# A three-stage kernel whose instruction order becomes a table over single instructions, with a named buffer for each place of a ring

## The chip, the core and the metric

The kernel runs on one core of one Trainium2 chip. The metric is the device time of one execution in microseconds (us), the median of several runs. The core has five queues of instructions that run beside each other, each in its own order: TensorE (PE, matrix products), VectorE (DVE), ScalarE (ACT), GpSimd (POOL) and SyncE (SP, which here issues all DMA transfers). An instruction that waits holds back everything behind it on its own queue.

## What is computed

An attention with a memory term, then two feed-forward networks, on 4 batches, 8 heads, 576 tokens and 64 values per head, so 2,304 rows of 512:

```python
scores = scale * q @ k.T, causal; a = softmax(scores); local = a @ v
q_p = phi(q); mem_out = (q_p @ M_prev) / (q_p @ z_prev + 1e-6)
x = sigmoid(beta) * mem_out + (1 - sigmoid(beta)) * local    # rows of 512
h = x @ w_in;  g = 0 | (h+1)**2/4 | h  by range;  x = g @ w_out        # 512 -> 2048 -> 512
h = x @ w2_in; g = max(h, 0) + alpha * min(h, 0); x = g @ w2_out
```

The weights arrive as 64-bit floats. Accuracy is kept by splitting: each operand of a product is a 16-bit high part and a 16-bit rest, and each product is done as three 16-bit products.

## The kernel before

Work is cut by batch b (0 to 3), by pairs of heads pr (0 to 3) and by two chunks of 288 tokens. The sections have short names: p0 prepares batch 0 (norms and scales), a0A1 is the attention of batch 0, pair 1, its first row blocks (B the later ones, C all), w1i, w1o, w2i and w2o are the four weights, u00 is the first product of the first network (batch 0, chunk 0, eight steps u00.0 to u00.7), d00 its second product, f00 the second network with steps f00.o0 to f00.o3 for its second product.

A weight comes in 16 raw pieces of 128x1024 words (512 KB). DVE and ACT turn two pieces into `w_t` (line 687 on), a product with ones gives a bound, then `copy` (line 516) makes the 16-bit high part on ACT, DVE or POOL, and `rest` (line 534) the 16-bit rest: on DVE one SCALAR_TENSOR_TENSOR, on POOL two instructions, a TENSOR_SCALAR over the source and a TENSOR_TENSOR. The same two helpers split q, k, v and the probabilities. In the networks, `split` does `copy` and `combine` (line 531, a subtraction on POOL or DVE) for the tile g.

All instructions are recorded first. `schedule` (line 273) then plays a list scheduler over estimated costs: each named part has a rank in the table RANK, each helper that could run on several engines may have its engine fixed in the table HOME, else the scheduler chooses, and the order in which it starts the instructions is the order in which they are issued (`run`, line 420). Tiles of one tag share a ring of equal places (`BUFS`, line 459: four for x, five for g, three for tmp, two for qk); a tile takes the place that is free when its turn comes. All instructions are issued from line 426.

Of the kernel before, what the change touches and what calls it, by code (L numbers as in the profile page):

```python
# [11 lines left out]
F32 = mybir.dt.float32  # L12
F32R = mybir.dt.float32r
F16 = mybir.dt.float16
# [29 lines left out]
class _Op:  # L44
    __slots__ = ("section", "first", "ways", "users", "before", "tiles", "size", "wide", "rows", "port", "key")
# [15 lines left out]
class _Pool:  # L61


    def __init__(self, plan, pool, name, bufs):
        self.plan, self.pool, self.name, self.bufs = plan, pool, name, bufs

    def tile(self, shape, dtype, tag=None, name=None, bufs=None):
        bufs = bufs or self.bufs
        if tag is None:
            ap = self.pool.tile(shape, dtype, name=name)  # L70
        else:
            ap = self.pool.tile(shape, dtype, tag=tag, name=name, bufs=bufs)
        self.plan.tiles[ap.tensor.name] = _Tile((self.name, tag or name), bufs)
        return ap


class _Tile:
    def __init__(self, group, bufs):
        self.group, self.bufs = group, bufs
        self.writes, self.reads, self.users = [], [], []  # L80


class Plan:

    NEAR, FAR, LAND = 0.14, 0.2, 0.8

    SLACK = 0.5

    def __init__(self, tc):
        self.tc = tc
        self.tiles = {}
        self.ops = []
        self.first = False
        self.joined = None
        self.turns = defaultdict(int)
        self.name = self.section = "c"  # L100

    def part(self, name):

        self.name = f"{self.section}.{name}"

    def pool(self, ctx, name, bufs, space=None):
        kw = {} if space is None else {"space": space}
        return _Pool(self, ctx.enter_context(self.tc.tile_pool(name=name, bufs=bufs, **kw)), name, bufs)

    @contextmanager  # L110
    def ahead(self):
        self.first = True
        yield
        self.first = False
# [8 lines left out]
    def either(self, *ways):  # L123
# [7 lines left out]
        self.turns[self.name] += 1  # L131
        first.key = f"{self.name}:{self.turns[self.name]}"
        if first.key in HOME:
            first.ways = {HOME[first.key]: first.ways[HOME[first.key]]}

    @staticmethod
    def cost(eng, method, out, ins, kw):

        w = max(math.prod(a.shape[1:]) for a in ((out, *ins) if method == "tensor_reduce" else (out,)))
        psum = any(a.space == PSUM for a in (out, *ins))  # L140
        scalars = sum(isinstance(kw.get(k), bass.AP) for k in ("scale", "bias", "scalar", "scalar1", "scalar2"))
        accum = kw.get("accum_out") is not None
        if eng == "act":
            extra = 0.054 + 0.094 * (scalars > 1) if psum else 0.1 * (scalars > 0)
            apart = 0.05 * any(a.ap[-1][0] == 2 for a in ins)
            return 0.1 + w / 1200 + extra + 0.09 * accum + apart
        if eng == "dve":
            if method == "tensor_tensor_reduce":
                return 0.078 + w / 960 + 0.06 * scalars
            if method == "reciprocal":  # L150
                return 0.09 + 0.006 * w
            rate = 1.04
            if not psum and not accum and method in ("tensor_scalar", "tensor_copy"):
                rate = 0.62 if out.dtype == F32 else 0.67 if out.dtype != I16 else 0.85
            small = 0.1 if w <= 8 else 0
            return 0.068 + w * rate / 1000 + 0.06 * max(psum, scalars) + small
        if method == "tensor_tensor":
            even = any(a.ap[-2][0] == 0 or a.ap[-1][0] == 0 for a in ins)
            return 0.148 + w * (1.667 if even else 1.886 if out.dtype == F16 else 2.103) / 1000
        if method == "tensor_scalar":  # L160
            return 0.161 + w / 1200 + 0.083 * (scalars > 0)
        return 0.3

    @staticmethod
    def two_ports(method, outs, ins, kw):

        big = [a for a in ins if a.space != PSUM and mybir.dt.size(a.dtype) == 4 and math.prod(a.shape[1:]) > 1]
        if method in ("tensor_scalar", "tensor_copy"):
            return bool(big) and outs[0].space != PSUM and kw.get("accum_out") is None
        return method in ("tensor_tensor", "scalar_tensor_tensor") and len(big) > 1  # L170

    @staticmethod
    def box(ap):

        n = mybir.dt.size(ap.dtype)
        dims = ap.ap
        if ap.space == bass.MemoryType.DRAM:
            lo = ap.offset
            return 0, 1, [(lo * n, (lo + 1 + sum(s * (c - 1) for s, c in dims)) * n, 0, 0)]
        row = dims[0][0]  # L180
        p0, lo = divmod(ap.offset, row) if row else (0, ap.offset)
        starts, size, step, width = [lo * n], n, 0, n
        for s, c in sorted(dims[1:], key=lambda d: abs(d[0])):
            if s == 0 or c == 1:
                continue
            if s * n > size and c * len(starts) <= 32:
                starts = [x + i * s * n for x in starts for i in range(c)]
                continue
            if s * n > size and len(starts) == 1:
                step, width = (s * n, size) if not step else (0, 0)  # L190
            size += s * (c - 1) * n
        return p0, p0 + dims[0][1], [(x, x + size, step, width) for x in starts]

    @staticmethod
    def overlap(a, b):
        def meet(r, q):
            if r[0] >= q[1] or q[0] >= r[1]:
                return False
            if r[2] and r[2] == q[2]:
                d = (q[0] - r[0]) % r[2]  # L200
                return d < r[3] or d + q[3] > r[2]
            return True

        return a[0] < b[1] and b[0] < a[1] and any(meet(r, q) for r in a[2] for q in b[2])

    def add(self, eng, method, fn, args, kw):
        aps = [a for a in args if isinstance(a, bass.AP)]
        outs = [kw[k] for k in ("out", "accum_out") if isinstance(kw.get(k), bass.AP)]
        ins = [v for k, v in kw.items() if isinstance(v, bass.AP) and k not in ("out", "accum_out")]
        if not outs:  # L210
            outs = aps[:1]
            aps = aps[1:]
        elif aps:
            raise ValueError(method)
        ins += aps
        if self.joined:
            op = self.joined
        else:
            op = _Op()
            op.section, op.first = self.name, self.first  # L220
            op.ways, op.users, op.before, op.tiles, op.rows, op.port, op.key = {}, [], 0, [], [], False, None
            self.ops.append(op)
            if self.joined is False:
                self.joined = op
        calls, cost = op.ways.setdefault(eng, ([], []))
        calls.append((fn, args, kw))
        if eng == "pe":
            if method == "transpose":
                cost.append(2 * P)
                op.rows.append(1.0)  # L230
            else:
                n = math.prod(kw["rhs"].shape[1:])
                whole = kw["rhs"].dtype == F32


                cols = math.prod(kw["lhsT"].shape[1:])
                if kw["lhsT"].shape[0] == 64 and whole:
                    cost.append(2 * n + 348)
                elif kw["lhsT"].shape[0] == 64:
                    cost.append(0.5 * n + (228 if kw["start"] and len(cost) < 2 else 6))  # L240
                elif cols == 64:
                    cost.append((2 if whole else 0.5) * n + (228 if kw["start"] and len(cost) < 2 else 6))
                else:
                    cost.append(max(4 * n, 300) if whole else n)
                op.rows.append(kw["lhsT"].shape[0] / P * (min(n, P) / P if whole else 1))
        elif eng == "dma":
            op.size = math.prod(outs[0].shape) * mybir.dt.size(outs[0].dtype)
            if "transpose" in method:
                op.size = -op.size
# [6 lines left out]
        for ap, writes in [(a, False) for a in ins] + [(a, True) for a in outs]:  # L256
            t = self.tiles.get(ap.tensor.name)
            if t is None:
                continue
# [1279 lines left out]
```

## Time and profile before

| | |
|---|---|
| time, median of 3 runs | 1032.7 us (1026.01 to 1033.71) |
| span of the profiled execution | 1028.9 us; its own time is not listed apart, the median lies 3.8 us above its span |
| instructions | 20,943 |
| PE busy | 934.1 us, 91% |
| DVE, ACT, POOL busy | 682.0, 525.0 and 357.0 us |
| chain that ended last | PE 52%, DVE 20%, ACT 9%, DMA 8%, POOL 5% |

The profile gives busy time by engine, tables by stretch of time, the instructions in order of time, and the chain of work that ended last, followed back from the last instruction. Every instruction has the line of the one place that issues it, so tiles tell them apart: `ring` and `w1o_raw` are raw weights, `s` scores, `e` the exponentials, `sm` their sums, `h` and `g` the network's inner values. `x3` counts instructions.

### The profile page before, as it was taken

The numbers are of one execution on the slowest core, as the hardware profiler recorded it, in microseconds if no ns is written. First come the engines' busy times: TensorE is split into PE (matmuls) and PEld (weight loads), VectorE is DVE, ScalarE is ACT, GpSimd is POOL, SyncE is SP. The second block draws the span as 40 slices with busy tenths as digits, with TensorE's granted clock in tenths as the row PEclk, the third lists the DMA queues.
The fourth block names the chain that finished last, engine by engine and source line by source line (L and its number), as shares of the span: only waits on it lengthen the run. The fifth ranks groups of instructions, "written<-read, shape, count | busy, mean of one in ns | idle before, by whom it ended". The sixth has DMA issues, their size and how long they took to land.

```text
span 1028.9 us, 20943 instructions
## 1 busy us (share of the span) xinstructions
PE 934.1 (91%) x8215; PEld 703.2 (68%) x8215; DVE 682.0 (66%) x1748; ACT 525.0 (51%) x1091; POOL 357.0 (35%) x382
## 2 busy tenths in 40 slices
PE   1557979998999999999899999999999999999998
PEld 0334656766766666776577777777777777777776
DVE  5977887799888899999879988872241313142230
ACT  7867777466655667356655555653232323132220
POOL 3433334476547566374524424131120200100010
PEclk9955889999999999999999999999999999999999
DMA  8934413457734957455565444321100000000000
GB/s 311 340 109 139 171 57 109 117 131 164 173 98 109 209 121 177 64 153 157 100 161 161 151 142 137 118 79 38 36 12 13 12 18 7 24 7 18 12 13 24
DMA packets 135171, 107.80 MB, mean 105 GB/s; under 512 B 98464, under 2 KB 113312, under 8 KB 135072
## 3 DMA queue, kind: packets, MB, share of 16 engines
q1 hardware_dynamic: 135072, 106.47, 36.8%
q8 instruction: 64, 1.05, 0.5%
q14 instruction: 35, 0.29, 0.1%
HBM read 70.27 MB, written 9.44 MB: 77 GB/s over the span
## 4 chain that ended last, share of the span: by engine, by line
PE 52%; DVE 20%; ACT 9%; DMA 8%; POOL 5%; issue 4%; SPq 1%; ACTq 0%; DVEq 0%; POOLq 0%
PE h L426 24%; PE o L426 18%; PE y L426 5%; DVE p L426 3%; DVE u L426 2%; DVE d L426 2%; DVE e L426 2%; PE px L426 2%; DMA w2i_raw<-in_w2i 2%; DVE g L426 2%; DMA pt<-p 2%; ACT e L426 2%; PE s L426 2%; SPq L426 1%; DMA qn<-in_qn 1%
## 5 line engine op out<-in xcount | busy, mean ns | idle before, releaser
L426 PE MATMUL h<-x,w1i 128*128 128x288 f16 x1536 | 203.6, 290 | 10.8 <-DVE u L426 10.1
L426 PE MATMUL y<-g,w1o 128*128 128x288 f16 x1536 | 202.4, 288 | 2.9 <-DVE u L426 2.5
L426 PE MATMUL h<-yt,w2i 128*128 128x288 f16 x1536 | 195.8, 286 | 2.9 <-ACT u L426 2.9
L426 PE MATMUL o<-g,w2o 128*128 128x288 f16 x1536 | 194.4, 286 | 0.1
L426 PEld LDWEIGHTS <-w1i 128*128 128x128 f16 x1536 | 148.3, 99 | 58.0 <-DVE u L426 15.3
L426 PEld LDWEIGHTS <-w1o 128*128 128x128 f16 x1536 | 146.1, 98 | 51.8 <-issue 10.1
L426 PEld LDWEIGHTS <-w2i 128*128 128x128 f16 x1536 | 150.3, 98 | 41.4 <-issue 3.7
L426 PEld LDWEIGHTS <-w2o 128*128 128x128 f16 x1536 | 150.2, 98 | 38.2 <-issue 0.4
L426 DVE SCALAR_TENSOR_TENSOR u<-u,al 128x288 f32<-128x288 f32 x128 | 64.7, 531 | 151.1 <-ACT u L426 151.0
L426 POOL TENSOR_TENSOR g<-u,g 128x576 f16<-128x576 f32 x50 | 70.1, 1403 | 154.9 <-ACT g L426 128.9
L426 ACT ACTIVATE u<-h,sa 128x288 f32<-128x288 f32 x128 | 59.2, 498 | 120.9 <-PE h L426 111.8
L426 POOL TENSOR_SCALAR g<-u 128x576 f16<-128x576 f32 x31 | 23.3, 753 | 253.6 <-DVE u L426 156.9
L426 DVE TENSOR_TENSOR g<-u,g 128x576 f16<-128x576 f32 x78 | 62.1, 798 | 70.8 <-ACT g L426 63.6
L426 ACT ACTIVATE e<-e,mxt 128x576 f32<-128x576 f32 (+4 forms) x160 | 88.1, 552 | 39.5 <-DVE mxt L426 36.9
L426 ACT ACTIVATE d<-d,bu,su 128x576 f32<-128x576 f32 x64 | 55.4, 865 | 51.2 <-DVE d L426 40.4
L426 PE MATMUL s<-qk 64*128 64x288 f16 (+9 forms) x528 | 66.8, 335 | 14.8 <-DVE mxt L426 8.5
L426 ACT ACTIVATE g<-u 128x576 f16<-128x576 f32 x75 | 51.1, 681 | 52.8 <-DVE u L426 36.4
L426 ACT ACTIVATE oe<-o,osc 128x288 f32<-128x288 f32 x32 | 16.0, 500 | 109.5 <-PE o L426 100.0
L426 DVE TENSOR_SCALAR d<-h,lim 128x576 f32<-128x576 f32 x64 | 55.6, 869 | 6.9 <-PE h L426 6.5
L426 DVE SCALAR_TENSOR_TENSOR p<-e,sm,p 128x192 f16<-128x192 f32 (+4 forms) x84 | 57.2, 707 | 1.1 <-ACT p L426 0.9
L426 DVE CUSTOM_DVE_ANT_0 e<-s,mask,qs 128x64 f32<-128x64 f32 (+4 forms) x120 | 54.7, 480 | 4.0 <-PE s L426 3.7
L426 DVE SCALAR_TENSOR_TENSOR u<-h,sd,d 128x576 f32<-128x576 f32 x64 | 52.0, 812 | 6.3 <-ACT d L426 5.3
(229 smaller groups left out, 1225.7 us busy)
## 6 DMA issues: line engine op xcount, KB each, us to landing
ring<-in_w1i SPq DMA_DIRECT2D x16, 512.0 KB, 6.2
w1o_raw<-in_w1o SPq DMA_DIRECT2D x16, 512.0 KB, 4.0
w2i_raw<-in_w2i SPq DMA_DIRECT2D x16, 512.0 KB, 4.1
w2o_raw<-in_w2o SPq DMA_DIRECT2D x16, 512.0 KB, 4.3
qr<-in_qk SPq DMA_DIRECT2D x24, 288.0 KB, 3.3
qn<-in_qn SPq DMA_DIRECT2D x16, 320.0 KB, 3.4
vc<-in_vc SPq DMA_DIRECT2D x16, 320.0 KB, 4.5
y<-ye SPq DMA_DIRECT2D x32, 144.0 KB, 2.4
```

Of the source, the lines that this page charges most:

```text
L426: fn(*args, **kw)
```

## The change

The recorded instructions are the same. The scheduler, its costs, RANK and HOME go. A table ISSUE lists the 3,795 recorded steps by number in the order in which they are issued, with a letter (a, v, g for ACT, DVE, POOL) where a step can run on several engines. A table PLACES gives each tile of a ring its place by name, as a buffer of its own with a fixed width.

```diff
-    def schedule(self, ops):
-        ...
-    def run(self, sections):
-        order, _ = self.schedule(...)
+    def run(self):
+        engines = dict(a="act", v="dve", g="pool")
+        order = ISSUE.split()
+        ...
+            for t in order:
+                op = self.ops[int(t.rstrip("avg"))]
+                eng = engines[t[-1]] if op.key else next(iter(op.ways))
+                for fn, args, kw in op.ways[eng]:
+                    fn(*args, **kw)
 ...
     def tile(self, shape, dtype, tag=None, name=None, bufs=None):
-        bufs = bufs or self.bufs
+        words, order = PLACES[f"{self.name}.{tag}"]
+        key = (tag, order[self.made[tag]])
+        self.made[tag] += 1
+        if key not in self.places:
+            self.places[key] = self.pool.tile([P, words], F32, tag="".join(key), name="".join(key), bufs=1)
 ...
-RANK = """
-w1i0.m1 w1i0.s0 s1 m1.0 p0.n c w1i0.m0 w1i1.m0 l p0.0 p0.2 a0A1.1 a0A1.2 a0A0.1 w1i2.m0 a0A0.0 w1i1.s1 a0A0.2 s0 p0.1
+    "sb.x": (1152, "3210011011001311231320300023320132013"),
+ISSUE = """
+1 40 5 2 6 0 34 22 13 70 7 41 72 42 43 69 23 8 9 35 44 186 36 28 24 10 37 1304 71 25 92a 11 45 26 76 12 18 91 187 38
```

Of the 980 steps that can run on several engines, 495 get another engine than before. Of the subtractions for g (`combine`), 41 go from DVE to POOL and 17 from POOL to DVE. Of the rests of weights, 12 go from POOL to DVE and 2 the other way. The order is close to the old one in the large and differs in the small nearly everywhere. Three places follow.

The first is SP's queue near the program's start, its DMA transfers 19 to 27; qk0_0_1 and qk0_0_0 are q and k of batch 0, pairs 1 and 0.

```order
L426 DMA w1o_raw0_0_324<-in_w1o 128x1024 [waits DMAHW2_49]
L426 DMA vc0_3_89<-in_vc 128x640 [waits DMAHW3_49,Activation_49]
L426 DMA w1o_raw0_1_325<-in_w1o 128x1024 [waits DMAHW4_49]
L426 DMA w1o_raw1_0_326<-in_w1o 128x1024 [waits DMAHW5_49]
L426 DMA qk0_0_1_176<-in_qk 128x2x320 [waits DMAHW6_49]
L426 DMA vf0_0_2_214<-in_vp 128x256 [waits DMAHW7_49]
L426 DMA vf0_0_2_214<-in_vp 64x384 [waits DMAHW0_49]
L426 DMA vf0_0_2_214<-in_vp 64x3x128 [waits DMAHW1_49]
L426 DMA qk0_0_0_137<-in_qk 128x2x320 [waits DMAHW2_49]
```

In the change the names are those of the places (wb0 to wb3 hold raw pieces of w1i, tmp0 a piece of vc); these are its transfers 12 to 22, where qk0 and qk1 are the same two loads of pairs 1 and 0.

```order
L135 DMA wb1_114<-in_w1i 128x1024 [waits DMAHW3_49]
L135 DMA tmp0_87<-in_vc 128x640 [waits DMAHW4_49,DVE_49]
L135 DMA qk0_146<-in_qk 128x2x320 [waits DMAHW5_49]
L135 DMA wb2_115<-in_w1i 128x1024 [waits DMAHW6_49]
L135 DMA wb3_116<-in_w1i 128x1024 [waits DMAHW7_49]
L135 DMA wb2_115<-in_w1i 128x1024 [waits DMAHW0_49]
L135 DMA vf0_145<-in_vp 64x384 [waits DMAHW1_49]
L135 DMA tmp2_88<-in_vc 128x640 [waits DMAHW2_49,DVE_49]
L135 DMA tmp0_87<-in_vc 128x640 [waits DMAHW3_49,Activation_49]
L135 DMA qn4_181<-in_qn 128x640 [waits DMAHW4_49]
L135 DMA qk1_128<-in_qk 128x2x320 [waits DMAHW5_49]
```

The load for pair 1 moved from the 23rd place on the queue to the 14th: four pieces of w1i, three of w1o and three of vc that stood ahead of it now stand behind it, and the load for pair 0 moved from 27th to 22nd.

The second place is SP's queue some thirty transfers later. Before, the fourth to sixth pieces of w1o wait for DVE, with q and k of batch 0, row block 3 (qk0_3_1) between them.

```order
L426 DMA qk0_0_3_254<-in_qk 128x2x320 [waits DMAHW5_49,PE_49]
L426 DMA vc1_2_518<-in_vc 128x640 [waits DMAHW6_49,DVE_49]
...
L426 DMA kc1_1_523<-in_qk 128x576 [waits DMAHW3_49,Activation_49]
L426 DMA w1o_raw1_1_327<-in_w1o 128x1024 [waits DMAHW4_49,DVE_49]
L426 DMA qk0_3_1_411<-in_qk 128x576 [waits DMAHW5_49,PE_49]
L426 DMA w1o_raw2_0_340<-in_w1o 128x1024 [waits DMAHW6_49,DVE_49]
```

In the change the same stretch reads so; x0, x1 and g0 to g3 here hold raw pieces of w1o, wb1 the last piece of w1i, and qk0 the load of pair 3.

```order
L135 DMA x1_171<-in_w1o 128x1024 [waits DMAHW7_49]
L135 DMA qk0_146<-in_qk 128x2x320 [waits DMAHW0_49,PE_49]
L135 DMA wb1_114<-in_w1i 128x1024 [waits DMAHW1_49]
...
L135 DMA g0_169<-in_w1o 128x1024 [waits DMAHW4_49]
L135 DMA vf1_127<-in_vp 64x384 [waits DMAHW5_49]
L135 DMA g1_162<-in_w1o 128x1024 [waits DMAHW6_49]
L135 DMA g2_166<-in_w1o 128x1024 [waits DMAHW7_49]
L135 DMA g3_168<-in_w1o 128x1024 [waits DMAHW0_49]
L135 DMA tmp2_88<-in_vc 128x640 [waits DMAHW1_49,Activation_49]
...
L135 DMA x1_171<-in_w1o 128x1024 [waits DMAHW3_49,DVE_49]
```

Four pieces of w1o that need no place to come free moved ahead of the first piece that waits for DVE; and the last piece of w1i, with those four, now stands behind the load of pair 3, which waits for PE.

The third place is POOL at the start, from its first products on; ph is phi(q) times z, w1i the 16-bit weights, pf the probabilities.

```order
L426 TENSOR_SCALAR w1i0_113<-w1i_t1_128,w1i1_s_133 128x1024
L426 TENSOR_SCALAR w1i_t1_128<-w1i_t1_128,w1i1_s_133 128x1024
L426 TENSOR_TENSOR w1i0_113<-w1i_t1_128,w1i0_113 128x1024
L426 TENSOR_TENSOR ph0_3_97<-qn0_3_96,zb0_83 128x640
L426 TENSOR_TENSOR pf0_0_1_2_199<-qn0_1_92,rn0_85 128x2x64
L426 TENSOR_TENSOR pf0_0_1_1_191<-qn0_1_92,rn0_85 128x2x64
L426 TENSOR_SCALAR w1i_t2_163<-w1i_t2_163,w1i2_s_168 128x1024
L426 TENSOR_TENSOR w1i1_114<-w1i_t2_163,w1i1_114 128x1024
```

In the change (tmp1 holds ph, wa1 and wa2 the 16-bit weights, p0 and p1 the probabilities, e and sm as before):

```order
L135 TENSOR_TENSOR tmp1_86<-qn3_90,zb0_83 128x640
L135 AFFINE_SELECT mask_79<-mask_79 128x128
L135 TENSOR_SCALAR wa1_109<-wt0_117,ws0_119 128x1024
L135 TENSOR_SCALAR p0_144<-e0_132,sm0_142 128x192
L135 TENSOR_TENSOR p0_144<-qn3_90,rn0_85 128x2x64
L135 TENSOR_SCALAR p1_133<-e1_143,sm1_149 128x320
L135 TENSOR_TENSOR p1_133<-qn3_90,rn0_85 128x2x64
L135 TENSOR_SCALAR wa2_110<-wt1_120,ws1_124 128x1024
```

The two-step rests of w1i left POOL; DVE has them now. Ahead of the first product of u00 there were four such pairs on POOL and there are none.

## Rows read from the trace of the kernel before

**Rows 1.** The page: busy time of an engine (share of the span) xinstructions
```profile
PE 934.1 (91%) x8215; PEld 703.2 (68%) x8215; DVE 682.0 (66%) x1748; ACT 525.0 (51%) x1091; POOL 357.0 (35%) x382
```
**Rows 2.** Busy time by stretch: length, each engine, clock share, DMA share, GB/s
```profile
0.00:103.00 103.00, 50.59 (x238) 32.73 (x239) 76.53 (x237) 78.13 (x169) 37.52 (x46) 0.76 0.64 225
103.00:161.00 58.00, 49.53 (x334) 34.34 (x333) 49.94 (x120) 45.59 (x79) 20.37 (x17) 0.86 0.35 114
161.00:640.00 479.00, 450.46 (x4526) 330.70 (x4522) 421.57 (x1121) 283.18 (x622) 253.27 (x281) 0.99 0.55 139
640.00:1029.00 389.00, 383.51 (x3125) 305.44 (x3123) 133.94 (x273) 118.14 (x223) 45.87 (x38) 1.00 0.09 30
```
**Rows 3.** The same columns (PE, PEld, DVE, ACT, POOL) for three short stretches
```profile
25.00:50.00 25.00, 13.41 (x52) 8.17 (x53) 23.38 (x61) 21.09 (x48) 12.79 (x12) 1.00 0.97 353
...
130.00:140.00 10.00, 6.15 (x41) 3.80 (x40) 9.44 (x24) 8.03 (x15) 5.61 (x4) 0.99 0.00 0
140.00:150.00 10.00, 9.33 (x45) 6.12 (x46) 6.70 (x23) 7.61 (x15) 1.71 (x3) 0.50 0.30 83
```
**Rows 4.** Chain that ended last, in order of time: start, length, what
```profile
36.58 2.45 POOL w1i L426
...
60.69 4.90 DMA qk<-in_qk
...
81.87 5.50 DMA w1o_raw<-in_w1o
...
102.75 4.42 PE h L426 x24
```
**Rows 5.** SP in order of time: start, length, transfer
```profile
22.31 0.69 SPq L426 DMA_DIRECT2D qk<-in_qk  x1
...
60.69 0.57 SPq L426 DMA_DIRECT2D qk<-in_qk  x1
...
65.47 0.38 SPq L426 DMA_DIRECT2D kc<-in_qk  x1
80.97 0.33 SPq L426 DMA_DIRECT2D w1o_raw<-in_w1o  x1
```
**Rows 6.** POOL in order of time: start, length, instruction
```profile
25.82 2.18 POOL L426 TENSOR_TENSOR w1i<-w1i_t,w1i 128x1024 f16<-128x1024 f32 x1
...
35.38 1.12 POOL L426 TENSOR_SCALAR w1i_t<-w1i_t,w1i_s 128x1024 f32<-128x1024 f32 x1 [1.38 <-DVE w1i L426]
36.58 2.44 POOL L426 TENSOR_TENSOR w1i<-w1i_t,w1i 128x1024 f16<-128x1024 f32 x1
...
94.90 2.13 POOL L426 TENSOR_TENSOR w1o<-w1o_t,w1o 128x1024 f16<-128x1024 f32 x1
```
**Rows 7.** DVE in order of time: start, length, instruction
```profile
25.94 2.74 DVE L426 SCALAR_TENSOR_TENSOR qn<-qn,ph 128x640 f32<-128x640 f32 x1
...
36.96 2.08 DVE L426 SCALAR_TENSOR_TENSOR sm<-sm,g1i 128x2 f32<-128x2 f32 x1
...
41.83 0.16 DVE L426 SCALAR_TENSOR_TENSOR sm<-sm,g1i 128x2 f32<-128x2 f32 x1
...
50.44 0.82 DVE L426 SCALAR_TENSOR_TENSOR qn<-qn,ph 128x640 f32<-128x640 f32 x1
...
84.67 1.28 DVE L426 SCALAR_TENSOR_TENSOR w1i<-w1i_t,w1i_s,w1i 128x1024 f16<-128x1024 f32 x1
...
95.05 3.07 DVE L426 SCALAR_TENSOR_TENSOR w1o<-w1o_t,w1o_s,w1o 128x1024 f16<-128x1024 f32 x1 [0.21 <-ACT w1o L426]
```
**Rows 8.** Groups of instructions by form: busy, mean ns of one, idle before
```profile
L426 DVE TENSOR_TENSOR g<-u,g 128x576 f16<-128x576 f32 x78 | 62.1, 798 | 70.8 <-ACT g L426 63.6 <-POOL g L426 6.9
L426 POOL TENSOR_TENSOR g<-u,g 128x576 f16<-128x576 f32 x50 | 70.1, 1403 | 154.9 <-ACT g L426 128.9 <-DVE g L426 15.3 <-DVE sm L426 4.9
```

More of the change, by code (lines that the diff above doesn't have):

```diff
@@ L1 @@
-import heapq
 import math
 import struct
-from collections import defaultdict, deque
+from collections import defaultdict
 from contextlib import ExitStack, contextmanager
@@ L44 @@
 class _Op:
-    __slots__ = ("section", "first", "ways", "users", "before", "tiles", "size", "wide", "rows", "port", "key")
+    __slots__ = ("ways", "key")
 class _Engine:
@@ L61, with __init__ @@
 class _Pool:
-    def __init__(self, plan, pool, name, bufs):
-        self.plan, self.pool, self.name, self.bufs = plan, pool, name, bufs
+    def __init__(self, pool, name):
+        self.pool, self.name = pool, name
+        self.made, self.places = defaultdict(int), {}
     def tile(self, shape, dtype, tag=None, name=None, bufs=None):
-        bufs = bufs or self.bufs
         if tag is None:
[L70 to L73, printed above, removed]
-        return ap
[L77 to L80, printed above, removed]
+            return self.pool.tile(shape, dtype, name=name)
+        words, order = PLACES[f"{self.name}.{tag}"]
[3 more added lines that the diff above has]
+            self.places[key] = self.pool.tile([P, words], F32, tag="".join(key), name="".join(key), bufs=1)
+        n = math.prod(shape[1:])
+        ap = self.places[key][0 : shape[0], 0 : -(-n * mybir.dt.size(dtype) // 4)]
+        if dtype != F32:
+            ap = ap.bitcast(dtype)
+        if len(shape) > 2:
+            dims = [f"d{i}" for i in range(1, len(shape))]
+            sizes = dict(zip(dims[1:], shape[2:]))
+            ap = ap.rearrange(f"p ({' '.join(dims)}) -> p {' '.join(dims)}", **sizes)
+        return ap
 class Plan:
-    NEAR, FAR, LAND = 0.14, 0.2, 0.8
-    SLACK = 0.5
     def __init__(self, tc):
         self.tc = tc
-        self.tiles = {}
         self.ops = []
-        self.first = False
         self.joined = None
[L99 to L104, printed above, removed]
     def pool(self, ctx, name, bufs, space=None):
         kw = {} if space is None else {"space": space}
[L108 to L114, printed above, removed]
+        return _Pool(ctx.enter_context(self.tc.tile_pool(name=name, bufs=bufs, **kw)), name)
     @contextmanager
@@ L130, in either @@
         self.joined = None
[L131 to L204, printed above, removed]
-    def add(self, eng, method, fn, args, kw):
[L207 to L218, printed above, removed]
+        first.key = True
@@ L219, in add @@
+    def add(self, eng, method, fn, args, kw):
+        op = self.joined
+        if not op:
             op = _Op()
-            op.section, op.first = self.name, self.first
-            op.ways, op.users, op.before, op.tiles, op.rows, op.port, op.key = {}, [], 0, [], [], False, None
+            op.ways, op.key = {}, False
             self.ops.append(op)
@@ L224, in add @@
                 self.joined = op
[L225 to L249, printed above, removed]
-            op.wide = op.size < 0 or len(outs[0].shape) > 3
-        else:
-            cost.append(self.cost(eng, method, outs[0], ins, kw))
-            if eng == "dve":
-                op.port = op.port or self.two_ports(method, outs, ins, kw)
@@ L255, in add @@
-        before = set()
[L256 to L259, printed above, removed]
-            if t not in op.tiles:
-                op.tiles.append(t)
-                t.users.append(op)
-            b = self.box(ap)
-            for other, o in t.writes + (t.reads if writes else []):
-                if other is not op and self.overlap(o, b):
-                    before.add(other)
-            (t.writes if writes else t.reads).append((op, b))
@@ L420, in run @@
-    def run(self, sections):
-        place = {name: i for i, name in enumerate(sections)}
-        order, _ = self.schedule(sorted(self.ops, key=lambda op: place.get(op.section, place.get(op.section.split(".")[0], -1))))
+        op.ways.setdefault(eng, []).append((fn, args, kw))
+    def run(self):
+        engines = dict(a="act", v="dve", g="pool")
+        order = ISSUE.split()
+        if sorted(int(t.rstrip("avg")) for t in order) != list(range(len(self.ops))):
+            raise RuntimeError("the order does not list every instruction once")
@@ L644, in groups @@
             w, inv = self.w, self.inv
-            plan.part("a")
             if self.bound is None:
@@ L699, in groups @@
                 for i in range(2):
-                    plan.part(2 * k + i)
                     raw = raws[2 * k + i]
@@ L785, in prepare @@
         for pr in range(NPAIR):
-            plan.part(pr)
             if halved:
@@ L825, in prepare @@
         rns = [rn[:, pr] for pr in range(NPAIR)]
-        plan.part("s")
         nm = 5 if halved else 2
@@ L877, in scale_memory @@
         for pr in range(NPAIR):
-            plan.part(pr)
             G.tensor_tensor(
@@ L917, in attend @@
             )
-        plan.part("q")
         if not plain:
@@ L959, in attend @@
             for run in runs:
-                plan.part(run[0][0])
                 ps = [
@@ L1079, in attend @@
             if bk in (2, 4):
-                plan.part(f"x{bk}")
                 for ch, (t0, n) in enumerate(CHS):
@@ L1265, in ffn2 @@
         for eb in range(EB):
-            plan.part(f"o{eb}")
             ps = psum.tile([P, 512], F32, tag="f", name=f"o{b}_{ch}_{eb}")
@@ L1317, in section @@
     def section(name):
-        plan.name = plan.section = name
         kind, num = name[0], name[1:]
@@ L1342 @@
         section(name)
-    plan.run(RANK)
+    plan.run()
 GTAGS = {}
```

539 lines of the change are left out of this document (262 added, 277 removed).

## The prediction

> **What bounds the kernel now.** I read the page's busy times first, then tables of busy time by stretch, then the chain that ended last, and then the instructions of single engines in order of time where the chain leaves PE. PE is busy for 934.1 of 1028.9 us [rows 1], so at most the 94.8 us in which it is idle, and what the half clock costs, can be won by an order. The stretches show where they lie [rows 2]. From 640 us on, the second network, PE works 383.5 of 389 us at full clock, with DVE, ACT and POOL under half used: there an order can win next to nothing. From 161 to 640 us PE works 450.5 of 479 us, idle 28.5, and DVE beside it 421.6 of 479. So in that stretch two engines are nearly full, and both have to be kept. In the first 161 us PE is idle for 52.4 + 8.5 = 60.9 us, two thirds of all, and its clock is 0.76 and 0.86 of full there. But DVE and ACT work 76.5 and 78.1 us of the first 103: the start is not idle, it is three engines and the DMA in turns. From 25 to 50 us the transfers run at 353 GB/s with a share of 0.97, and DVE is busy for 23.4 of 25 us [rows 3]. The chain of the start goes through single weights, loads and POOL, and reaches the first step of the first network at 102.75 us [rows 4].
>
> **The change, part by part.** The instructions are the same, so every term is a wait that gets shorter or longer. I take four, and leave the second network at 0 (5.5 us of PE idle there is all it has).
>
> First, the loads. Two legs of the chain are transfers that it had to wait for: 4.90 us for q and k of pair 3 and 5.50 us for a raw piece of w1o, 10.4 us together [rows 4]. Behind them stands SP: the load of pair 3 goes out at 60.69, and after 65.47 nothing is issued until 80.97, 15.5 us, because a piece of w1o waits for its place, which DVE has to free [rows 5]. The change puts the first load of q and k ahead of seven 512 KB weight pieces and three 320 KB pieces of vc, 4.65 MB, which at 353 GB/s [rows 3] is 13 us of transfer; before it was issued at 22.31 [rows 5]. And four pieces of w1o that need no wait now stand ahead of the blocked one. What hides a part of this is that DVE, which must take in the scores, is full from 25 to 50 us [rows 3]: earlier scores push other DVE work back. The gain lies between 0 (DVE is the limit anyway) and 10.4 us (both legs gone). I take 6, nearer to the upper end, since two legs stand on the chain itself. Queued behind the new waits: the last piece of w1i and four of w1o behind the load of pair 3, which waits for PE; that is the third rival.
>
> Second, POOL's rests at the start. Four two-step rests stand on POOL ahead of the first network and all go to DVE. A pair takes 1.12 + 2.44 us on POOL [rows 6] and one instruction of 1.28 us on DVE [rows 7], so DVE gets 5.1 us more. In return it waits less: while POOL ran its subtraction, DVE's qn step took 2.74 us instead of 0.82, its tiny sm step 2.08 instead of 0.16, and its own rest 3.07 instead of 1.28 [rows 6, 7], 1.92 + 1.92 + 1.79 = 5.6 us for three of the four pairs. On DVE's time alone that is a gain of 0.5 us. One pair lies on the chain with 2.45 us for its second step [rows 4], where 1.28 would stand, and its first step of 1.12 us goes as well: 2.3 us. Bounds: +5.1 us if the stalls stay, since other POOL work fills the time, and -5.6 if the added rests fall into the 26.5 us in which DVE is idle before 103 [rows 2]. I take -2, the chain's figure.
>
> Third, the clock. From 140 to 150 us PE is busy for 9.33 us at half clock, 0.50; in the 10 us before it had been busy for 6.15 us only, while DVE was at 9.44 [rows 3]. At full clock the same products would need 4.7 us. If PE is fed more evenly through 130 to 140, these 4.7 us go; if the change makes another such hole, they come again. Bounds -4.7 and +4.7; I take -2, because ahead of the first network the DVE work is pulled forward and less of it is left for this stretch.
>
> Fourth, the middle, 161 to 640 us. Net 24 subtractions for g move from DVE (0.80 us each) to POOL (1.40 us) [rows 8], over the middle and the second network. DVE saves 19.2 us and POOL takes 33.7. POOL gives up rests of weights, q, k and v in exchange, so that its sum stays near 357 us, and DVE's near 682. With both sums as they were, only the waits between engines are left: PE's 28.5 us. I take -2. Bounds: -8 (a quarter or so of PE's idle time), and +14.5 if each of the 24 stops DVE for its full 1.40 us: 33.7 - 19.2.
>
> On the stalls, the rows show 2.08 us for a step that takes 0.16 alone, started 0.38 us after a POOL instruction of 2.44 us and ended with it [rows 6, 7]. The Trainium skill, page SBUF — State Buffer, section "Who interferes with whom", says that VectorE with two SBUF inputs and GpSimd share a port pair that is locked for a whole instruction, so that the second one fully blocks. The trace agrees in these rows. Were every POOL rest at the start to cost DVE its full 3.56 us, the second term would be 4 x 3.56 - 5.1, a gain of 9.1 us, but the same lock would make the fourth term +14.5; the sum by that is -6 - 9.1 - 2 + 14.5 = -2.6, which is the second rival. The rows lie between: of four pairs, three show a stall, of under 2 us each.
>
> The sum: -6 - 2 - 2 - 2 = -12 us. The profiled span is 1028.9 us, which gives a span near 1017; its own time is not listed apart from it. Set against the median of the runs, 1032.7, that is 3.8 us above the span, it gives 1020.7, say 1020 us.
>
> **The rivals.** One: the start is really won. PE's 60.9 idle us before 161 [rows 2] are halved, since loads, stalls and clock feed each other there. That gives 1032.7 - 30 = about 1003 us. For it speaks that the chain before 103 us is made of many short waits, against it that DVE and ACT already work three quarters of that time and their sums don't fall.
>
> Two: nothing is left over. The new order only moves work along a DVE that is the limit from 25 us on [rows 2, 3]; what the start wins, POOL's locks on the 24 moved subtractions take back, and the sum is the -2.6 us above: 1030 us. For it speaks that all engine sums stay, against it the two transfer legs on the chain. That the change does not do what it says can't be: order and engines stand in the built program.
>
> Three, slower: SP's queue stops at the load of pair 3. It waits for the scores of pair 1's last block to be done on PE; before, it went out at 60.69 us [rows 5] with four w1o pieces already loaded. In the change the last w1i piece and four w1o pieces stand behind it, 5 x 512 KB, 7.4 us at 353 GB/s [rows 3]. The first network's first product stands on PE behind w1o's bound. If this load goes out at about 60 us the pieces are there by 70 and nothing is late. From about 70 us on every us is added: at 80 us the weights come 10 us late, and these 10 stand in place of the 6 won: -2 - 2 - 2 + 10 = +4, and 10 more with the half clock that a wait of PE has brought here before (0.50 after the thin stretch [rows 3], 4.7 us in each of two such stretches). That is 1046 us. Against it: the scores of pair 1 start earlier in the change, so this wait should end earlier too.
>
> **How the numbers follow.** I give the forecast 0.37, the first rival 0.13, the second 0.33 and the third 0.17. The predicted time is the forecast's, 1020 us. Two runs of this kernel can be told apart from about 1% on, 10.3 us: faster means under 1022.4, slower over 1043.0. The forecast and the first rival lie under, 0.50; the second between, 0.33; the third above, 0.17. The forecast's own terms reach from 1004 (10.4 + 5.6 + 4.7 + 8 us off) to 1057 (0, +5.1, +4.7, +14.5). For 8 in 10 I cut at 1001, which leaves out 0.05 of the first rival, and at 1042, which leaves out 0.15 of the third. The forecast's own range is 1010 to 1028.
>
> **What would show it.** In the profile of the change: the first load of q and k issued before 16 us, and no gap of SP over 8 us between 60 and 85; the chain with less than 5 us of transfers before the first network; qn and sm steps of DVE at 0.82 and 0.16 us before 50 us; POOL busy for under 30 us in the first 103; the first product of the first network before 100 us; the clock at 1.00 through the stretch that follows; PE's sum from that stretch to the second network unchanged but for 2 to 4 us of idle. Wrong would be: DVE above 80% through the first 100 us with the first network no earlier (second rival), or the load of pair 3 after 70 us (third), or DVE's subtractions and other two-input steps longer on average than 798 ns with more POOL beside them.

## The result: 984.75 us, and the profile after

The changed kernel takes 984.75 us (median of 4 runs, 983.53 to 988.43), the one before 1032.5 us (four runs on the same occasion): a ratio of 0.955 with a 95% interval from 0.951 to 0.9595, so 48 us faster. I had forecast 1020 us, with a range from 1001 to 1042. The sign was right. The size was wrong by a factor of nearly four, and the time lies below the range. The profiled execution took 984.8 us, its span 982.9.

The page of the changed kernel, the busy times (it answers to [rows 1]):

```profile
PE 920.6 (94%) x8215; PEld 699.2 (71%) x8215; DVE 654.1 (67%) x1733; ACT 511.2 (52%) x1079; POOL 339.2 (35%) x400
```

Every sum has shrunk: PE by 13.5 us, DVE by 27.9, ACT by 13.8, POOL by 17.9. The prediction held DVE's and POOL's sums to be fixed.

To compare equal work, I cut both traces at the same products: the first of the first network, the first of its second weight, and the first of the second network. The cut between the last two stretches is not exact: about a dozen products that stand behind it before stand ahead of it in the change, an estimated 1.5 us at 390 us for 3,185 products. The next rows are the table by stretch, first of the kernel before, then of the change. The columns are those of [rows 2]: length, PE, PEld, DVE, ACT, POOL, clock, DMA share, GB/s.

```profile
0.00:102.60 102.60, 50.19 (x236) 32.47 (x237) 76.36 (x235) 77.77 (x168) 37.52 (x46) 0.77 0.64 224
102.60:174.20 71.60, 61.81 (x450) 43.42 (x451) 60.68 (x171) 57.90 (x105) 26.63 (x26) 0.88 0.36 116
174.20:629.40 455.20, 429.62 (x4335) 314.93 (x4335) 403.49 (x1060) 264.54 (x587) 242.94 (x271) 0.99 0.56 138
629.40:1029.00 399.60, 392.47 (x3197) 312.39 (x3195) 141.46 (x283) 124.83 (x233) 49.94 (x41) 1.00 0.10 34
```

```profile
0.00:93.60 93.60, 47.94 (x236) 31.05 (x237) 68.50 (x244) 76.28 (x162) 21.88 (x33) 0.80 0.74 251
93.60:154.70 61.10, 56.26 (x451) 40.39 (x451) 54.47 (x152) 52.65 (x100) 35.08 (x35) 0.98 0.37 117
154.70:589.20 434.50, 426.27 (x4348) 316.79 (x4348) 378.99 (x1043) 269.75 (x601) 223.10 (x281) 1.00 0.63 145
589.20:983.00 393.80, 390.10 (x3185) 310.98 (x3182) 152.16 (x297) 112.57 (x219) 59.12 (x51) 1.00 0.11 36
```

The four stretches gained 9.0, 10.5, 20.7 and 5.8 us, 46.0 together, the whole difference of the spans. The middle, the third stretch, gave the most. There PE's idle time fell from 25.6 to 8.2 us, and DVE's busy time from 403.5 to 379.0 us, while DVE's idle time stayed (51.7 and 55.5 us). What PE waited for from 155 to 640 us, in the view of waits (who waits for whom: us in total, times, longest), before and then in the change:

```profile
PE h L426 <- DVE u L426: 7.7, 9, 1.4
PE px L426 <- DMA pt<-p: 5.8, 5, 1.9
PE s L426 <- DVE mxt L426: 3.5, 6, 1.9
PE px L426 <- DVE x L426: 2.8, 4, 1.0
PE y L426 <- DVE u L426: 2.5, 4, 1.0
```

```profile
PE px L135 <- DVE x L135: 3.0, 2, 2.4
PE px L135 <- DMA tt<-p: 2.7, 4, 1.2
PE f L135 <- DVE u L135: 1.6, 3, 1.0
PE s L135 <- DVE mxt L135: 0.6, 3, 0.2
```

The waits for u, the DVE step that frees a product of the first network, were 10.2 us and are 1.6; `f` is now the place that held h and y. The first places of SP's queue that the prediction spoke of (SP in order of time, answers to [rows 5]):

```profile
13.00 0.59 SPq L135 DMA_DIRECT2D qk<-in_qk  x1
...
55.46 0.57 SPq L135 DMA_DIRECT2D qk<-in_qk  x1
...
64.50 0.33 SPq L135 DMA_DIRECT2D vf<-in_vp  x1
75.37 1.37 SPq L135 DMA_DIRECT2D x<-in_w1o  x2
```

And legs of the chain that ended last, up to the first network (answers to [rows 4]):

```profile
22.06 5.51 DMA tmp<-in_vc
...
43.57 3.98 DMA tmp<-in_vc
...
85.01 4.94 DMA g<-in_w1o
...
93.75 4.43 PE f L135 x24
```

The loads go out 9.3 us earlier for pair 1 and 5.2 for pair 3, yet the chain still goes through three transfers of 4 to 5.5 us, two of them of vc, which were not on it before, and SP still has a hole of 10.5 us (64.83 to 75.37).

### The profile page after: what moved, and what is told of

Read it like the earlier page. It is cut to its first block, busy times and chain, and to the rows that moved or that the text cites. A ratio compares the mean times of both kernels' runs of the same rounds, so it can differ in the third digit from the quotient of the medians.

```text
span 982.9 us, 20948 instructions
## 1 busy us (share of the span) xinstructions
PE 920.6 (94%) x8215; PEld 699.2 (71%) x8215; DVE 654.1 (67%) x1733; ACT 511.2 (52%) x1079; POOL 339.2 (35%) x400
## 4 chain that ended last, share of the span: by engine, by line
PE 63%; DVE 13%; DMA 10%; ACT 6%; POOL 3%; issue 3%; SPq 1%; DVEq 0%; ACTq 0%; POOLq 0%
PE f L135 59%; DMA tt<-p 5%; PE s L135 3%; DVE e L135 3%; DVE p L135 2%; PE px L135 2%; POOL p L135 2%; SPq L135 1%; DVE d L135 1%; DVE wt L135 1%; DVE u L135 1%; ACT e L135 1%; DMA tmp<-in_vc 1%; DMA al<-in_alpha 1%; ACT wb L135 1%
## 5 line engine op out<-in xcount | busy, mean ns | idle before, releaser
L135 PEld LDWEIGHTS <-wa 128*128 128x128 f16 x3072 | 298.5, 98 | 83.9 <-issue 7.7
L135 PE MATMUL f<-g,wb 128*128 128x288 f16 x1536 | 200.5, 287 | 1.3 <-DVE u L135 1.3
L135 PE MATMUL f<-x,wa 128*128 128x288 f16 x1536 | 199.4, 287 | 1.1 <-DVE u L135 1.0
L135 PE MATMUL f<-g,wa 128*128 128x288 f16 x1536 | 191.9, 286 | 0.0
L135 PEld LDWEIGHTS <-wb 128*128 128x128 f16 x1536 | 146.6, 98 | 46.6 <-issue 8.0
L135 POOL TENSOR_TENSOR g<-u,g 128x576 f16<-128x576 f32 x74 | 99.8, 1353 | 207.2 <-ACT g L135 107.9
L135 PEld LDWEIGHTS <-vf 128*64 128x64 f16 (+1 forms) x1656 | 88.0, 106 | 31.5 <-issue 16.1
L135 ACT ACTIVATE e<-e,mxt 128x64 f32<-128x64 f32 (+4 forms) x160 | 88.1, 551 | 28.3 <-DVE mxt L135 28.0
L135 PE MATMUL f<-x,e 128*128 128x288 f16 x576 | 75.5, 286 | 0.0
L135 PE MATMUL f<-x,vf 128*128 128x288 f16 x576 | 75.1, 286 | 0.0
L135 PEld LDWEIGHTS <-qk 64*128 64x128 f16 (+1 forms) x816 | 51.7, 96 | 25.1 <-issue 11.3
L135 PE MATMUL px<-tt,vf 128*64 128x128 f16 (+2 forms) x1320 | 59.5, 238 | 10.1 <-ACT tt L135 3.8
L135 PEld LDWEIGHTS <-e 128*128 128x128 f16 x576 | 56.4, 98 | 14.2
```

What stands on the lines that cost most here:

```text
L135: fn(*args, **kw)
```

## Experiments: order, engines, places

The change is three things in one: an order, a choice of engines for 495 steps, and a named place for each tile. All kernels here are issued from the new table; where the order is another one, each tile takes the place that came free first. The runs fall on several occasions, and on these the median of the kernel before lay between 1029.0 and 1032.6 us, so differences of 2 or 3 us between kernels of different occasions mean little.

**n1, only the named places.** Order and engines as before; the table's start shows it:

```diff
-1 40 5 2 6 0 34 22 13 70 7 41 72 42
+0 6 1 1304 3 2 22 4 5 34 7 28 8 1305
```

> The order and the engines of before, issued from the new table, each ring tile in a named buffer (the place that came free first). Theory P (the named buffers bring the gain, since a tile no longer takes its place by turn): 985 to 1000 us. Theory O (the order brings it) and theory E (the choice of engines brings it): the time of before, 1027 to 1036 us, PE idle near 95 us.

Measured 1035.0 us, ratio 1.0045 (1.0022 to 1.0068): a trace slower than before. With the order of before the places win nothing, so theory P falls. n1 is what the following are compared with, where they use the order of before.

**n2 and n3, order and engines apart.** n2 has the change's order with the old letters:

```diff
-204 99 101v 15 233 155a 102v 236a
+204 99 101g 15 233 155a 102g 236a
```

> The order of the change, but each of the 495 steps that changed engine is back on the engine of before; places as in the change. Theory O: 980 to 1000 us, since the 46 us come from the order. Theory E: 1020 to 1045 us, DVE's sum back near 680 us and POOL's near 357 us, PE idle near 90 us. If the two belong together (an order made for its own engines), slower than before, over 1043 us.

n3 has the order of before with the new letters:

```diff
-1308 463 170v 101g 19 87v
+1308 463 170a 101v 19 87v
```

> The order of before with the engines of the change; named places. Theory E: 985 to 1005 us, DVE's sum near 654 us. Theory O: 1020 to 1040 us. If the two belong together: over 1043 us, with DVE's two-input steps stalled by POOL and a sum of DVE above 690 us.

Measured 1055.6 us (ratio 1.025, 1.022 to 1.027) and 1049.5 us (1.019, 1.016 to 1.022). Neither theory O nor theory E holds. Each half alone is slower than before, by 25 and 19 us, and both together are 48 us faster. Both times lie over 1043 us, as expected for the case that the two belong together; DVE's sum above 690 us, expected for n3 in that case, did not come: it is 678.9. The middle of n2 and of n3, cut at the same products:

```profile
175.20:651.60 476.40, 434.97 (x4349) 319.67 (x4349) 403.60 (x1064) 262.82 (x589) 241.67 (x274) 0.99 0.58 132
```

```profile
177.60:652.10 474.50, 435.24 (x4337) 319.08 (x4335) 400.82 (x1034) 270.69 (x600) 224.89 (x280) 0.99 0.57 134
```

DVE is as busy as before (403.6 and 400.8 us, before 403.5) and idle for 73 us instead of 52 or 55; PE is idle for 41 and 39 us. The low DVE sum of the change is therefore neither the doing of the engines alone nor of the order alone.

**n4, n7, n8, stretches apart.** The table is cut: one order up to a step, the other behind it.

> The change's order and engines up to the first product of the first network (its first 490 steps), the rest in the order and on the engines of before. In the traces of before and of the change this product starts at 102.6 and 93.6 us. Theory S (the earlier start carries on: with the weights and scores ready, the rest has more room): more than 9 us, 1005 to 1018 us. Theory M (every stretch has its own gain, 9 us here, 8 to the end of the first batch, 26 in the middle): 1020 to 1026 us. Theory L (a lead at the start is lost again, the middle is limited by DVE): 1028 to 1035 us.

> The first 770 steps as before (to the last attention step of batch 0, near 168 us), all later ones in the order and on the engines of the change. Theory M (each stretch has its own gain: 9 us to the first network, 8 to the end of the first batch's attention, 26 to the second network, 3 in it): 1001 to 1009 us. Theory S (the middle's gain needs the lead of the start): over 1018 us.

> The other part: the first 870 steps as in the change (to near 169 us), all later ones in the order and on the engines of before. Theory M: 1012 to 1018 us, the 17 to 20 us of the start kept to the end. Theory L2 (a lead is lost again in a middle that DVE limits): over 1022 us.

Measured 1025.6 (n4), 1006.9 (n7) and 1019.2 us (n8). Against n1's 1035.0 the start alone wins 9.4 us, the first two stretches 15.8, the rest without them 28.1. The last two make 43.9 of the 50.2 us between n1 and the change. n8 lies 1 us above what theory M said, the others within it: every stretch has its own gain, to some 6 us, and n7 has its 28 us with the first network starting at 103.4 us, as late as before.

## Experiments: what carries the middle

**n5 and n6, POOL's two-input steps taken out** of n1 and of the change.

```diff
-fn(*args, **kw)
+if eng == "pool" and fn.__name__ == "tensor_tensor" and math.prod(kw["out"].shape[1:]) >= 192:
+    self.two_scalars(fn.__self__, kw["out"], kw["in0"], kw["in1"])
```

> The order and engines of before with named buffers, but each two-input instruction of POOL of 192 elements or more is two one-input instructions on the same tiles that together last about as long alone. The rests and products that POOL makes are left out by that (it copies instead). In the traces DVE's two-input steps beside a two-input step of POOL last 0.2 to 0.7 us longer on average, beside a one-input step 0.03 to 0.15. Theory L (in the middle DVE is the limit, and its stalls beside POOL, about 82 us in all and 52 in the change, make the difference): 990 to 1012 us, DVE's sum near 615 us, and the gap to the change without them under 25 us. Theory W (PE's waits come from the order of the steps, stalls go into DVE's idle time): 1022 to 1034 us, the gap stays over 38 us.

> The change with the same replacement on POOL; the same parts are left out. Theory L: 968 to 982 us, since only 52 us of stalls are there to be won, DVE's sum near 610 us. Theory W: 978 to 986 us, less than 6 us below the change.

Measured 1024.4 us for n5, 10.6 below n1, and 987.9 us for n6, 3 us above the change and not clear of its noise (ratio 0.958, 0.9556 to 0.9603, against 0.955). The pages of the two:

```profile
PE 929.1 (91%) x8215; PEld 701.8 (69%) x8215; DVE 658.6 (65%) x1748; ACT 524.9 (52%) x1091; POOL 367.6 (36%) x519
```

```profile
PE 920.3 (94%) x8215; PEld 699.0 (71%) x8215; DVE 643.0 (65%) x1733; ACT 511.9 (52%) x1079; POOL 350.1 (36%) x548
```

DVE's sum fell by 23.1 us in n5 (from 681.7) and by 11.1 in n6, though DVE does the same steps and POOL works 11 us longer. That these were stalls beside POOL's two-input steps is shown by this. But of 23.1 us only 10.6 came off the time, and of 11.1 nothing. The gap between the two orders was 50.2 us and is 36.5 without these steps: between the 25 of theory L and the 38 of theory W, close to W. n5's time lies in W's range, n6's 2 us above it, and both far above L's. In the middle alone, n1 takes 460.3 us, n5 451.6 and the change 434.5. So the stalls that these steps cause make up to 14 us of the gain, some 9 of them in the middle. Not all stalls are gone, and what the last of them cost stays open.

**n9 and n10, groups of engines.** n9 puts back the letters of g alone:

```diff
-545a 543v 425a 441 460a 426g 415 562
+545a 543v 425g 441 460a 426v 415 562
```

> The change with only the 139 steps that make the tile g back on the engines of before (58 subtractions, 81 copies); order and all other engines as in the change. n2, all 495 steps back, cost 71 us against the change. Theory F (an order fits the engines that it was laid out for; every step put elsewhere stands at the wrong place of another queue, whatever the step): 139 of 495 steps, 15 to 30 us, 1000 to 1015 us. Theory G (the choice for g carries the middle, since DVE is freed by it): 1020 to 1045 us.

n10 puts back all others (the diff is that of n2).

> The complement: the other 356 changed steps (probabilities, weights, q, k, v, raw pieces) back on the engines of before, g as in the change. Theory F: 40 to 60 us over the change, 1025 to 1045 us. Theory G: under 15 us over it, below 1000 us.

Measured 1002.6 us (n9, 18 over the change) and 1054.3 us (n10, 70 over it). Theory G falls. Theory F's figure holds for n9 and is too low for n10: the 356 steps cost as much as all 495.

**n11 and n12, the order of single engines.** A piece of POOL's queue, the change and n12:

```diff
-1508g 1509g 1433g 1504g 1438g 1875g 1525g 1524g 1528g 1903g
+1853g 1508g 1509g 1504g 1433g 1438g 1525g 1903g 1524g 1528g
```

> The change's engines and its order on PE, ACT and SP; on DVE and POOL the steps stand in the relative order of before, as far as the data allow (neighbours out of the change's order: 598 on DVE, 89 on POOL, none elsewhere). Theory D (the middle is won by the order on DVE, which serves the products of the first network sooner: in the traces 0.77 us from the end of a product to its first reader before, 0.48 us in the change): 1015 to 1045 us, and that wait back above 0.7 us. Theory T (PE's and SP's order wins, DVE's order is only the shadow of it): below 1000 us.

> The same with POOL alone in the relative order of before (83 neighbours on POOL out of the change's order, none on another engine). Theory D: within 10 us of the change, 980 to 995 us. If POOL's order carries the gain (its two-input steps beside DVE's): over 1000 us, DVE's sum above 665 us.

Measured 1358.7 and 1054.8 us. n11 decides nothing between D and T: two queues laid out for one order and three for another wait for each other until PE is busy for 75% only. n12 falls outside theory D's range: 83 neighbours out of order among POOL's steps, on an engine that is busy a third of the time, cost 70 us. The other branch had the time right and its reason wrong: DVE's sum was to rise above 665 us, and it is 654.0, the change's own 654.1. So the low DVE sum is there without any of the gain. In the middle of n12 PE waited 15.0 us for the transposed probabilities and 12.8 for u, in the change 2.7 and 1.6. POOL's idle time is no slack as long as its queue is in order and others wait for what it makes.

**n13 and n14, DVE's steps d and u by two places.** n13 brings them forward in n1's order, n14 puts them back in the change (808 is a d):

```diff
-909 792 1027v 961 954 808 963 793
+909 792 808 1027v 954 961 963 793
```

> The order and engines of before (as n1, 1035 us), but from the second chunk of batch 0 on the two DVE steps that read a product of the first network (d and u) stand two DVE steps earlier. Theory U (the middle was won because DVE frees the products sooner): 1015 to 1028 us, product end to last reader's end under 3.5 us. Theory F (no single class of steps carries it, the whole order fits together): within 6 us of n1 or slower, 1030 to 1050 us.

```diff
-793 954 808 809 975 1750 902 769
+793 954 1750 975 769 902 808 809
```

> The change with the same two DVE steps two DVE steps later, from the second chunk of batch 0 on. Theory U: 997 to 1015 us, product end to last reader's end over 3.7 us. Theory F: 985 to 995 us (a small class moved by a little costs little).

Measured 1069.8 us (n13, 35 over n1) and 1028.6 us (n14, 44 over the change). n14 goes the way of theory U, but costs 44 us where theory U had 12 to 30; n13 goes against it, and lies above theory F's figure too. The waits tell why. In n14, PE and what it waits for from 155 to 640 us:

```profile
PE f L135 <- DVE u L135: 32.2, 26, 4.2
PE px L135 <- DMA tt<-p: 3.3, 3, 1.2
```

In n13, DVE and what it waits for there:

```profile
DVE u L135 <- ACT d L135: 24.9, 28, 3.0
DVE d L135 <- PE f L135: 15.2, 16, 2.3
```

Two places late, and PE stands for u, 32.2 us in place of 1.6. Two places early, and DVE stands at the head of its queue for ACT and PE, 40.1 us in place of 8.6 in n1 (3.6 and 5.0), with everything behind it. From the end of a product to the end of its last reader it takes 3.37 us in the change (mean over the 56 products after the first chunk), 3.66 before, 5.09 in n14 and 3.96 in n13, where the steps were meant to be earlier. This figure alone does not set the time: n14, with 5.09, is 41 us faster than n13, with 3.96. What the two runs show is that in either order these steps stand where two places more or less cost 35 to 44 us.

## Experiments: the start

**n15 and n16 undo one priced move each.** n15, the loads of q and k (187 is pair 1):

```diff
-18 91 187 38 77a 151 73 1305
+18 91 151 38 77a 153 73 1305
```

> The change with the loads of q and k of batch 0, pairs 1 and 0, back on the 23rd and 27th place of SP's queue (14th and 22nd in the change). The prediction's first term, 6 us of the chain: 989 to 993 us. If DVE or the weights set the start: 983 to 987 us.

n16, the four weight rests:

```diff
-233 155a 102v 236a
+233 155a 102g 236a
```

> The change with the four weight rests that stood on POOL ahead of the first network before back on POOL, as two steps each. The prediction's second term, 2 us: 985 to 989 us. If the stalls behind them count in full (4 x 3.56 us - 5.1 us): 990 to 996 us.

Measured 990.75 us (6.0 over the change, as expected) and 993.5 us (8.7 over it, where 2 were expected; it lies in the range for stalls in full). The first network starts at 97.6 and 99.1 us, 4.0 and 5.5 us later than in the change: together 9.5, about the 9.0 that the start has won. The rest of the 6.0 and 8.7 comes later, and the runs don't say where from. The stretch of n16 up to there:

```profile
0.00:99.10 99.10, 48.98 (x236) 31.27 (x237) 68.27 (x240) 76.15 (x162) 35.29 (x41) 0.78 0.70 238
```

Four rests of 1.28 us have left DVE, 5.1 us, and yet DVE is as busy as in the change (68.3 and 68.5 us): with 240 steps in place of 244, the others have grown by 4.9 us, stalls by the argument of n5. Three of the four rests belong to w1i and one to w1o. Two of them stand on n16's chain, each as two steps of POOL:

```profile
27.22 1.15 POOL wt L135
...
28.45 2.63 POOL wa L135
...
34.86 1.58 POOL wt L135
...
36.51 2.13 POOL wa L135
```

That is 7.5 us where two steps of 1.28 would stand on DVE: 4.9 us of the 5.5 by which the first network starts later.

**n17 and n18, products of zeros in PE's waits,** to see what the half clock costs between 50 and 95 us.

```diff
+for j, (tag, n) in enumerate([("px", 40), ("px", 12), ("px", 6), ("px", 21), ("f", 3), ("f", 25), ("f", 4), ("f", 4), ("s", 11)]):
...
+            for _ in range(n):
+                T.matmul(fill[:, 0:288], lhsT=mask[:, 0:128], rhs=mask[:, 0:288], start=True, stop=True)
```

> The change with 126 products of zeros that nobody reads, put on PE into nine of its waits between 24 and 93 us (0.7 of each wait as long as the trace of the change shows it, at full clock). If the half clock from 50 to 95 us lies on the path (PE busy 33 us there at about half clock) and the fill keeps it full: 974 to 981 us. If the chain there is loads, weights and DVE: 983 to 987 us. If the fill stays at half clock and lasts twice as long: 988 to 995 us.

> The same with 30 more such products between 54 and 86 us, five every 2.5 us or more. If the fill of n17 is too thin to keep the clock: this one 974 to 981 us. If the chain there is loads, weights and DVE: 984 to 990 us.

Measured 987.7 us (ratio 0.9588) and 986.1 us (0.9567), no better than the change (0.955). n17 lies between the two upper ranges, n18 in the one for loads, weights and DVE. In n18 the fill did what it was for:

```profile
50.00:91.60 41.60, 31.50 (x240) 21.20 (x241) 35.41 (x142) 36.24 (x83) 7.87 (x12) 0.96 0.59 197
91.60:155.00 63.40, 56.54 (x467) 40.99 (x468) 57.18 (x165) 53.68 (x101) 35.12 (x35) 1.00 0.35 113
```

The clock is 0.96 where the change has 0.57, and the first network starts 2.0 us earlier, at 91.6. The next stretch then takes 63.4 us instead of 61.1. The half clock at the start is not what bounds the time. n15 and n16 show that loads and weight rests bound it in part; that DVE does is argued from what is left and was not tried. No kernel tried beats the change.

## Why the prediction was right in sign and wrong in size

**First term, loads, -6: the size fits, the picture only in part.** n15 gives 6.0, of which 4.0 lie ahead of the first network. It undoes only the two loads of q and k; the four pieces of w1o that moved ahead, the other half of the term, no run puts back. Pair 1's load went out before 16 us, but the hole of SP and the transfers on the chain stayed, against what I had listed as signs: of the two legs that were to go, that of pair 3 is gone, that of w1o is still there with 4.94 us, and two loads of vc, 5.51 and 3.98 us, are new. That the figure fits is in part luck.

**Second term, weight rests, -2: mis-sized.** It measured -8.7 (n16), outside my bounds, of which 5.5 lie ahead of the first network. I had read one pair of four on the chain, 2.3 us; in n16 two stand there, 4.9 us. I had named the price with every rest at its full 3.56 us on DVE, 4 x 3.56 - 5.1 = 9.1, but as stalls; n16 shows 4.9 us of them, not 14.2, so that the 9.1 comes near the 8.7 is chance. The Trainium skill, page SBUF — State Buffer, section "Who interferes with whom", says that who comes second on the shared port pair is fully blocked. n16 (4.9 us) and n5 (23.1 us) agree that DVE's steps grow beside POOL's two-input steps; that every rest meets such a step, no run shows. The two terms made 8 us; at the first product 9.0 were won.

**Third term, clock, -2: mis-sized.** Between the first network and its second weight 10.5 us were won. PE's busy time fell by 5.5 (clock 0.88 to 0.98) and its idle time by 5.0, and I had counted no idle time there. I had also taken it that products halve at full clock, 9.33 us to 4.7. They shrink less: the scores of 64x288 took 764 ns at 0.50 before and 455 in the change, the transposes of the probabilities 403 and 279, so of the 9.33 us some 3.6 were to be won, an estimate from these rows. A part of the clock's share may be chance, since each stretch is read from one execution: n1, with the order of before, had a clock of 0.94 and 68.2 us in this stretch.

**Fourth term, the middle, -2: the step that failed.** It measured -20.7, and my lower bound was -8, "a quarter or so of PE's idle time". The reasoning was "with both sums as they were, only the waits between engines are left". Two things were wrong in it. The quarter had no row behind it: of 25.6 us of PE's idle time 17.4 went, two thirds. The waits of PE in the middle stood in the trace, 10.2 us of them for u alone, which has to read a product before the next one may take its place; the change kept 1.6. And the sums did not stay: DVE's 403.5 us in the middle held stalls beside POOL. Matched step by step over both traces, the 1347 steps that are on DVE in both take 576.9 us before and 557.3 after; the steps exchanged make 8.3 us more. But this was the smaller part: by n5 the stalls are worth some 9 us of the middle, and n12 has the change's DVE sum without its time. Why the waits went, beyond that, the runs don't show.

**Second network, 0.** It gave 5.8 us: PE's idle time fell from 7.1 to 3.7 us, its busy time by 2.4. Some 1.5 us of it belong to the middle, by the inexact cut.

**The rivals.** The first (the start is really won, 1003 us) had the right side but the wrong place: 19.5 us came ahead of the middle and 26.5 in it and behind it. The second let POOL's locks on 24 moved subtractions take back what the start wins. They did not: DVE's subtractions for g last 801 ns on average, before 798 [rows 8], and POOL's 1353 instead of 1403. The third, SP standing at the load of pair 3, did not occur: it went out at 55.46 us.

**What stays open.** Of the 50 us between n1 and the change, the stalls beside POOL make up to 14 and the start and the second stretch about 16, partly the same ones. Which other part of the order carries what is left in the middle, the runs don't isolate. They show that none of the classes tried can be moved alone: the engines of g, the engines of the rest, POOL's order and the two DVE steps cost 18 to 70 us each (n9, n10, n12, n14), the two small moves at the start 6 and 9.

## What to carry to other kernels

An engine's busy sum is not its work: here it held stalls that another order removed, so equal sums of steps are no floor. Nor is a low sum a gain, as n12 shows. In this kernel order and engine choice were one thing, to be laid out and changed together: 112 steps two places off their spot in one queue cost 44 us, nearly all that the table brought. To price a new order, read who PE waits for in the busiest stretch and ask of each wait whether the data or only the place in a queue makes it; a share of the idle time taken by feel is not a bound.

## Of the hardware, not expected

POOL's two-input steps slow DVE far more than one-input steps that do as much: replacing them made POOL work 11 us longer and DVE 23.1 us shorter (n5). With the change's order DVE's sum fell by 11.1 us (n6).

The granted clock that the tables show for the start is not always the one that the products had. They show 1.00 up to about 50 us in most runs, and up to 100 us in n5, n7 and n13, and yet the products there last as long as at half clock. These are the transposes of the probabilities, in n1 between 50 and 102 us, where the table says 0.51, in n7 there, where it says 1.00, and in n18 between 50 and 91 us, where it says 0.96:

```profile
L135 PE MATMUL f<-ident,p 128*128 128x128 f32 x34 | 9.6, 433 | 2.4 <-ACT p L135 2.4
L135 PE MATMUL f<-ident,p 128*128 128x128 f32 x34 | 9.6, 434 | 2.4 <-ACT p L135 2.4
L135 PE MATMUL f<-ident,p 128*128 128x128 f32 x34 | 6.5, 313 | 1.7 <-POOL p L135 0.9 <-DVE p L135 0.4 <-ACT p L135 0.4
```

Before 50 us it is the same: the scores of 64x320 took 817 ns in the kernel before between 14 and 50 us, where the table says 1.00, and 481 in n18 between 50 and 91. So a clock share has to be checked against the length of a product, and the 0.76 to 0.80 of the first stretch are too high. That n7 starts the first network at 103.4 us and n1 at 104.6 says nothing of the clock, which was the same.
